# Key blocks loaded a period ahead: issued on GpSimd's queue, and at pieces 6 to 8 of the feed-forward

## The chip, the cores and the metric

The kernel runs on one core of a Trainium2 chip. The metric is the device time of one execution in microseconds. A core has engines that work side by side and meet through semaphores: TensorE (PE in the profile, its weight loads PEld), VectorE (DVE), ScalarE (ACT), GpSimd (POOL) and SyncE (SP). Each of them works its own list of instructions in order. SP does nothing but issue DMAs; ACT and POOL issue some too, between their computing instructions.

## The reference

Two stages. The first is a gated linear attention (delta rule) over 4 batches, 8 heads, 768 positions and head dimension 48, the second a feed-forward layer on the 3072 tokens that it gives.

```python
k_n = k / (np.linalg.norm(k, axis=-1, keepdims=True) + 1e-06)
for t in range(S):
    y[:, :, t] = einsum('bhd,bhde->bhe', q[:, :, t], state)
    v_old = einsum('bhde,bhd->bhe', state, k_n[:, :, t])
    state = state + beta_t * einsum('bhd,bhe->bhde', k_n[:, :, t], v[:, :, t] - v_old)
x = y.transpose(0, 2, 1, 3).reshape(B * S, H * D)          # 3072 x 384
h = np.maximum(np.maximum(x @ w1, x @ w2), x @ w3)         # 3072 x 768
out = h @ w_out                                            # 3072 x 384
```

The weights come as 64-bit floats and are turned to 32 bits on the chip.

## The kernel before

The positions are cut into 12 chunks of 64. A chunk has two units (two batches each), so there are 24 units, and a group is 4 units, that is two chunks: six groups, and six token tiles of 512. Within a chunk the recurrence becomes small matrix products: transposed keys and queries of a unit (`turn`, later `turn_blocks`), their products (`gram`), a triangular solve that VectorE does row by row for a whole group (`solve`, L569 and L573), and then the steps that carry the state from chunk to chunk (`old_k`, `old_q`, `new`, `step`, `to_y`).

The order of all work is written out by hand. The feed-forward of token tile m (`ffn(m)`) is a generator that yields after each of its pieces: for m of 1 to 5, pieces 0 to 11 are the hidden layer (6 blocks of two products, p_h, L927), and 12 to 19 are the four output blocks (p_o, L959, each with a copy o_sb on ACT and two stores on SP, L968). After each piece the loop at the end of the kernel calls `links`, which looks up in the table `LINKS` what else is emitted there for the groups behind: letters name functions, digits the unit or chunk. One pass of that loop, one m, is called a period here.

These letters matter for what follows:

- `y1`, `x1`, `w1`, `X1`: the attention output of a period's second chunk. `to_y` makes y (L813 on DVE), `y_blocks` stores it to a scratch tensor in DRAM (two DMAs on SP, L843), `read_y` reads it back rearranged into the tile qall (four DMAs on SP, L854), and `turn_y` transposes it on DVE into xt (L865). The first product p_h of the next period reads xt. `y0` to `X0` are the same for the first chunk.
- `L3`, `N0`, `N1`, `N2`: `load_blocks` for the four units of a group. It loads 32-row blocks of k and of q into two tiles, each after a small memset on GpSimd (L395), with 8 DMAs of 48 KB for k and 8 for q (L400). `N0` to `N2` serve the group after the next, `L3` the next one. The k blocks are issued by SP, the q blocks by GpSimd. Units whose number leaves 2 by division by 4 use the tiles kmore; the other units share five buffers named turned.
- `t0` to `t3`: `turn_blocks`, the DVE transposes (L416) that read these tiles and free their buffers.
- `P0`, `P1`: `prep_values`, a GpSimd multiplication of the values v_t (L292), which `old_k` of the next period needs (L755).
- `g0` to `g3`: after the product, part of the result goes to DRAM (at_d, L472, on SP) and comes back as x_bl (L519, on SP) for the next solve.

`N0` to `N2` do something only in the periods m=1 and m=2; in m=3 the group that they would serve no longer exists, while everything else of m=3 is as in m=2. The units 12 to 14 are loaded by direct calls in the first feed-forward, not by `N`.

SP's list in the second half of period m=1 has this order: x_bl, 8 key blocks of N0, y_x of the first chunk, qall, 8 key blocks of N1, two output stores, 8 key blocks of N2, y_x of the second chunk, two output stores, qall, four output stores, then the result of the solve (L595, L604).

Of the kernel before, what the change touches and what calls it, by code (L numbers as in the profile page):

```python
# [21 lines left out]
def kernel(  # L22
# [31 lines left out]
    nc = tc.nc  # L54
# [73 lines left out]
    def load_k(n, queues=one_queue):  # L128
        load(k, kpad[place(n)], n, queues)

    def load_q(n, queues=one_queue):
        load(q, qpad[n % NQ], n, queues)

    def load_v(c, queue=nc.sync):
        vts[c] = work.tile([128, 2, H, D], FP32, name="v_t", bufs=3)
        for bb in range(2):
            queue.dma_start(
                out=vts[c][rows(bb)].rearrange("p g h d -> p (g h) d"),
                in_=v[2 * bb : 2 * bb + 2, :, c * C : (c + 1) * C, :].rearrange(
                    "b h p d -> p (b h) d"  # L140
                ),
            )
# [66 lines left out]
    def fetch(queue=nc.scalar):  # L209
        if fetched[0] < len(pieces):  # L210
            _, src, (a, b) = pieces[fetched[0]]
            st = work.tile([128, 2 * 384], U32, name="w_bits", bufs=5)
            queue.dma_start(
                out=st.rearrange("p (a b) -> p a b", a=a), in_=src
            )
            staged.append(st)
            fetched[0] += 1
# [79 lines left out]
    def prep_values(c):  # L297

        scale(c, nrms.pop(c))
# [49 lines left out]
    def turn(n, parts=(0, 1), copy=nc.scalar.copy):  # L349

        if n not in kqts:
            if n == 6:
                kqts[n] = work.tile([128, KT, TOK], FP32, name="xt").rearrange(
                    "p k t -> p (k t)"
                )[:, 0 : NP * 4 * C].rearrange(
                    "p (j b i t) -> p j b i t", b=2, i=2, t=C
                )
            else:
                kqts[n] = work.tile([128, NP, 2, 2, C], FP32, name="kqt", bufs=6)
        kqt = kqts[n]  # L360
        p_t = ps_two("p_t")
        for i in parts:
            src = (kpad[place(n)], qpad[n % NQ])[i]
            for j in range(NP):
                nc.tensor.transpose(
                    p_t[:, i, j * 128 : (j + 1) * 128],
                    src[:, 2 * j : 2 * j + 2],
                    ident,
                )
        some = slice(parts[0], parts[-1] + 1)  # L370
        copy(  # L371
            kqt.rearrange("p j b i t -> p i (j b) t")[:, some],
            p_t.rearrange("p i (x t) -> p i x t", t=C)[:, some],
        )
# [6 lines left out]
    TURNED = 32 + NP * 2 * D + 16  # L381
    turned = {}

    def load_blocks(n):
        c, g = divmod(n, 2)
        for i in range(2):
            if n % 4 == 2:
                t = kmore[i].rearrange("p a h d -> p (a h d)")[:, 0 : 2 * TURNED]
                t = t.rearrange("p (b x) -> p b x", b=2)
            else:  # L390
                t = work.tile(
                    [128, 2, TURNED], FP32, name="turned", tag="w_bits", bufs=5
                )
            turned[n, i] = t
            nc.gpsimd.memset(t[:, :, TURNED - 48 : TURNED], 0.0)  # L395
            for bb in range(2):
                for par in range(2):
                    for db in range(2):
                        p0, at = DP * par + 32 * db, 32 * (1 - db)
                        (nc.sync, nc.gpsimd)[i].dma_start(  # L400
                            out=t[p0 : p0 + 32, bb, at : at + NP * 2 * D].rearrange(
                                "p (j x) -> p j x", j=NP
                            ),
                            in_=(k, q)[i][
                                2 * bb + g, :, c * C : (c + 1) * C, :
                            ].rearrange(
                                "(j two) (r tb) d -> two r j (tb d)", two=2, tb=2
                            )[par],
                        )
# [21 lines left out]
    def gram(n, parts=(0, 1), queues=one_queue, copy=nc.scalar.copy, later=False):  # L431
        kqt, g = kqts[n], n % 2
        p_g = ps_two("p_g")

        whole = len(parts) == 2 and not g
        for j in range(NP):
            for par in range(2):
                for bb in range(2):
                    kq = kqt[dims(par), j, bb ^ g]
                    for i in (0,) if whole else parts:  # L440
                        c0 = j * 128 + i * C
                        nc.tensor.matmul(  # L442
                            p_g[
                                rows(bb ^ (g * i)), par, c0 : c0 + C * (1 + whole)
                            ],
                            kq[:, 0],
                            kq if whole else kq[:, i],
                        )
        p_v = p_g.rearrange("p two (j i t) -> p two j i t", j=NP, i=2)
        if 1 in parts:  # L450
            pt = pts[n] = square("pt")
            if later:
                copy(by_par(pt), p_v[:, :, :, 1])
            else:
                masked(pt, p_v[:, :, :, 1])
        if 0 not in parts:
            return
        at = ats[n] = square("at")
        copy(by_par(at), p_v[:, :, :, 0])
        if queues:  # L460
            to_dram(n, queues)
# [511 lines left out]
    def some(gen, n):  # L973
        for _ in range(n):
            if next(gen, gen) is gen:
                break
# [72 lines left out]
    for c in range(2):  # L1049
# [29 lines left out]

    LINKS = {  # L1080
        0: "k0 q0 t0 L3", 1: "g0 t1", 2: "g1 t2", 3: "z0 d0 g2", 4: "z1 d1 t3",
        5: "j0 g3", 6: "j1", 7: "u0", 8: "s0", 9: "y0 N0", 10: "k1 q1 x0",
        11: "w0 N1 V0", 12: "u1", 13: "K0 K1 N2", 14: "y1 x1 X0 V1", 15: "s1 w1",
        16: "K2 K3 P0", 18: "X1 P1",
    }
    EARLY_LINKS = {
# [15 lines left out]
        e=halves_z, f=halves_u, d=turn_t1,  # L1102
    )
    MADE = dict(V=load_v, P=prep_values)
    UNIT = dict(t=turn, g=gram, K=load_k, L=load_blocks)
    OF_KEYS = dict(S=lambda n: some(solving, n), T=lambda n: turn(n, (1,)), P=lambda n: gram(n, (1,)))

    def links(m, names):
        for name in names.split():
            f, i = name[0], int(name[1])  # L1110
            if f in RECURS and m < GROUPS:
                RECURS[f](2 * m + i)
            elif f in MADE and m + 1 < GROUPS:
                MADE[f](2 * (m + 1) + i)
            elif f in UNIT and m + 1 < GROUPS:
                UNIT[f](4 * (m + 1) + i)
            elif f == "N" and m + 2 < GROUPS:
                load_blocks(4 * (m + 2) + i)

    def queries(names):  # L1120
        for name in names.split():
            f, n = name[0], int(name[1])
            if f not in OF_KEYS:
                links(0, name)
                continue
            OF_KEYS[f](n)
            if f == "T" and n + 3 < 11:
                load_q(n + 3)
# [4 lines left out]
    for i, _ in enumerate(ffn(0)):  # L1133
        if i - 1 in CONVERTED:
            fetch(nc.sync)
        queries(FIRST.get(i, ""))
        links(1, EARLY_LINKS.get(i, ""))
        if i in CONVERTED:
            some(conv, 1)
        if i in (4, 5, 6):  # L1140
            some(solving, (4, 2, 1)[i - 4])
        if i in (5, 7):
            prep_values(i // 2)
        if 7 <= i < 11:
            load_k(i + 1)
        if i == 0:
            load_v(3)
        if i == 12:
            load_q(11)
        if i in (10, 18):  # L1150
            load_v(4 + i // 18)
        if i == 18:
            blocks(2)
        if i == 21:
            solving = solve(2)
            some(solving, 1)
        if i in (22, 25):
            prep_values(4 + i // 25)
        if 21 < i < 27:
            some(solving, 3)  # L1160
        if i >= 27:
            some(solving, 4 if i < 30 else 5)
        if i in (27, 28, 29):
            load_blocks(i - 15)
        if i in (18, 19, 20, 22, 25, 27):
            less_first((18, 19, 20, 22, 25, 27).index(i))
        if 27 <= i < 30:
            turn_first((2 * (i - 27), 2 * (i - 27) + 1))


    RECURS.update(x=y_blocks, w=read_y, X=turn_y)
    UNIT.update(t=turn_blocks, K=lambda n: load_k(n, (nc.scalar, nc.scalar)))
    MADE.update(V=lambda c: load_v(c, nc.scalar))
# [45 lines left out]
```

## Time and profile before

| | |
|---|---|
| median of three runs | 565.05 us (562.16, 565.05, 565.74) |
| profiled execution, its own time | 563.47 us |
| profiled execution, span | 561.6 us |
| PE busy | 512.9 us (91%) |
| DVE busy | 312.8 us (56%) |
| ACT busy | 154.7 us (28%) |
| POOL busy | 127.6 us (23%) |
| mean granted TensorE clock | 0.95 |

The profile is one execution. Its times are microseconds from the start of the span. A group row gives an engine, an operation and its tiles, with the number of instructions and the busy time. In a timeline, a line is a run of like instructions: start, duration, engine, source line, tiles, count, and in brackets how long the engine had stood idle before, and whom it waited for. "PEclk" is the share of full speed that the clock of TensorE was granted. Rows of SPq, POOLq and ACTq are DMA issues or waits of those queues.

### The profile page before, as it was taken

The page shows a single profiled execution, that of the slowest core. Times are in us where ns is not written, and L with a number is a line of the kernel's source. Part 1 is how long each engine was busy: PE and PEld are TensorE (multiplying, and loading weights), DVE is VectorE, ACT ScalarE, POOL GpSimd, SP SyncE. Part 2 cuts the span into 40 slices and gives each one's busy share as a digit, 9 for nine tenths or more (in the row PEclk, how much of TensorE's full clock was granted, in tenths as well). Part 3 has the DMA queues.
Part 4 walks back from the last instruction along what each step waited for, and adds up shares of the span by engine and source line. Part 5 has one row for each costly group of instructions (what it writes and reads, how often), then busy time and mean ns, then how long its engine had stood idle before and what let it go on. Part 6 is the DMA issues. An engine that isn't in the chain of part 4 may idle for free.

```text
span 561.6 us, 18516 instructions
## 1 busy us (share of the span) xinstructions
PE 512.9 (91%) x8096; PEld 313.5 (56%) x8096; DVE 312.8 (56%) x694; ACT 154.7 (28%) x285; POOL 127.6 (23%) x219
## 2 busy tenths in 40 slices
PE   6568878899899999999599999599999999999996
PEld 5457667766446555556255556255565555654453
DVE  6878898668898350588163688262798212101000
ACT  4555455393303233210024200124201231011100
POOL 6215236144490533011066011030011000000000
PEclk9855799999989999999799999799999999999999
DMA  8884556975035744057474267551165400130001
GB/s 114 176 163 113 110 145 143 186 158 130 2 78 114 159 85 111 8 123 145 114 138 80 68 132 145 117 98 29 50 137 115 91 2 30 45 91 7 0 19 37
DMA packets 147455, 53.48 MB, mean 95 GB/s; under 512 B 131696, under 2 KB 143792, under 8 KB 147376
## 3 DMA queue, kind: packets, MB, share of 16 engines
q1 hardware_dynamic: 116784, 42.37, 35.0%
q10 hardware_dynamic: 27264, 5.11, 5.0%
q0 software_dynamic: 3328, 4.83, 3.9%
q8 instruction: 63, 1.03, 0.8%
q14 instruction: 16, 0.13, 0.1%
HBM read 39.17 MB, written 13.11 MB: 93 GB/s over the span
## 4 chain that ended last, share of the span: by engine, by line
PE 64%; DVE 15%; DMA 9%; SPq 5%; issue 3%; ACT 3%; POOL 0%; DVEq 0%; ACTq 0%; POOLq 0%
PE p_h L927 32%; PE p_o L959 15%; DMA y_x<-y 5%; PE p_g L442 3%; DVE tmp L569 3%; SPq L118 2%; DVE y_bl L573 2%; PE p_m L907 2%; SPq L854 2%; PE p_k L743 2%; PE p_j L726 2%; PE p_y L811 1%; PE p_q L743 1%; PE p_u L771 1%; PE p_s L793 1%
## 5 line engine op out<-in xcount | busy, mean ns | idle before, releaser
L927 PE MATMUL p_h<-xt,w_sb 128*128 128x512 f32 (+1 forms) x522 | 227.7, 578 | 18.1 <-DVE tmp L569 12.5
L927 PEld LDWEIGHTS p_h<-xt,w_sb 128*128 128x128 f32 x522 | 97.1, 197 | 103.1 <-issue 94.4
L959 PE MATMUL p_o<-wo_sb,h 128*128 128x384 f32 x288 | 99.4, 490 | 0.0
L941 DVE TENSOR_TENSOR h<-h,p_h 128x512 f32<-128x512 f32 (+1 forms) x48 | 29.6, 617 | 86.2 <-PE p_h L927 86.2
L959 PEld LDWEIGHTS p_o<-wo_sb,h 128*128 128x128 f32 x288 | 53.5, 190 | 35.9 <-issue 2.4
L569 DVE TENSOR_TENSOR tmp<-x_bl,y_bl 128x31 f32<-128x31 f32 (+20 forms) x139 | 52.6, 379 | 3.9
L573 DVE TENSOR_TENSOR y_bl<-y_bl,tmp 128x31 f32<-128x31 f32 (+20 forms) x139 | 48.6, 350 | 4.8
L292 POOL TENSOR_TENSOR v_t<-v_t,nrm 128x768 f32<-128x768 f32 x12 | 18.6, 1556 | 142.8 <-DMA v_t<-in_v_dram 75.8
L965 ACT COPY o_sb<-p_o 128x384 f32<-128x384 f32 x24 | 11.5, 478 | 130.8 <-PE p_o L959 86.0
L937 ACT ACTIVATE h<-p_h 128x512 f32<-128x512 f32 x30 | 17.9, 597 | 90.2 <-PE p_h L927 88.8
L959 PE MATMUL p_o<-w_sb,xt 128*128 128x384 f32 x120 | 42.0, 486 | 0.0
L400 POOL DMA_DIRECT2D turned<-in_q_dram x72 | 39.1, 551 | 3.0 <-POOL turned L395 3.0
L442 PE MATMUL p_g<-kqt 48*64 48x64 f32 (+1 forms) x1216 | 29.2, 237 | 10.6 <-DVE nt_bl L268 3.8
L442 PEld LDWEIGHTS p_g<-kqt 48*64 48x64 f32 x1216 | 24.3, 137 | 18.1 <-ACT kqt L371 7.8
L959 PEld LDWEIGHTS p_o<-w_sb,xt 128*128 128x128 f32 x120 | 22.8, 190 | 15.9
L426 DVE TENSOR_TENSOR pt<-p_g,mask 128x512 f32<-128x512 f32 x22 | 15.2, 690 | 24.1 <-PE p_g L442 23.9
L865 DVE STREAM_TRANSPOSE xt<-qall 128x768 f32<-128x768 f32 x8 | 9.7, 1212 | 25.6 <-DMA qall<-y_x 25.6
L236 POOL TENSOR_SCALAR mant<-mant 128x384 f32<-128x384 f32 x24 | 13.5, 562 | 43.3 <-ACT mant L232 43.3
L755 DVE TENSOR_TENSOR v_t<-v_t,p_k 128x768 f32<-128x768 f32 x11 | 10.4, 949 | 22.4 <-PE p_k L743 22.4
L799 DVE TENSOR_TENSOR st<-st,p_s 128x768 f32<-128x768 f32 x11 | 10.5, 951 | 21.1 <-PE p_s L793 21.1
L259 POOL TENSOR_TENSOR w_sb<-mant,up 128x384 int32<-128x384 int32 x18 | 17.9, 996 | 12.7 <-DVE mant L255 12.7
L395 POOL MEMSET turned<- 128x96 f32 x18 | 3.1, 187 | 77.3 <-DVE kqt L416 49.8
(147 smaller groups left out, 579.8 us busy)
## 6 DMA issues: line engine op xcount, KB each, us to landing
w_bits<-in_moe_w_dram SPq DMA_DIRECT2D x18, 384.0 KB, 4.7
out_dram<-o_sb SPq DMA_DIRECT2D x48, 96.0 KB, 2.2
turned<-in_q_dram POOLq DMA_DIRECT2D x72, 48.0 KB, 2.5
turned<-in_k_dram SPq DMA_DIRECT2D x72, 48.0 KB, 3.1
y_x<-y SPq DMA_DIRECT2D x16, 192.0 KB
qall<-y_x SPq DMA_DIRECT2D x32, 96.0 KB, 2.5
kpad<-in_k_dram ACTq DMA_DIRECT2D x28, 96.0 KB, 3.3
at_d<-at SPq DMA_DIRECT2D x80, 32.0 KB, 1.9
```

The source lines that it names most:

```text
L259: nc.gpsimd.tensor_tensor(out=dst.bitcast(I32), in0=mant_v.bitcast(I32), in1=up_v, op=ALU.add)
L292: nc.gpsimd.tensor_tensor(out=vts[c], in0=vts[c], in1=nrm[:, :, :, None].to_broadcast([128, 2, H, D]), op=ALU.mult,)
L400: (nc.sync, nc.gpsimd)[i].dma_start(out=t[p0 : p0 + 32, bb, at : at + NP * 2 * D].rearrange("p (j x) -> p j x", j=NP), in_=(k, q)[i][2 * b ...
L426: engine.tensor_tensor(out=by_par(t), in0=of, in1=mask[:, None, None, :].to_broadcast([128, 2, NP, C]), op=ALU.mult,)
L442: nc.tensor.matmul(p_g[rows(bb ^ (g * i)), par, c0 : c0 + C * (1 + whole)], kq[:, 0], kq if whole else kq[:, i],)
L569: nc.vector.tensor_tensor(out=t_v, in0=row.to_broadcast(t_v.shape), in1=column.to_broadcast(t_v.shape), op=ALU.mult,)
L573: nc.vector.tensor_tensor(out=rest, in0=rest, in1=t_v, op=ALU.subtract)
L743: nc.tensor.matmul(p_b[rows(bb), par, c0 : c0 + D], kqt[g][dims(par), j, bb ^ g, i], st[dims(par), bb ^ g, g, j],)
L927: nc.tensor.matmul(p_h, w_sb[i][:, t, f * 128 : (f + 1) * 128], xt[:, t, lo : lo + w], start=(t == 0), stop=(t == KT - 1),)
L937: nc.scalar.activation(out=h, in_=p_h, func=mybir.ActivationFunctionType.Relu)
L941: nc.vector.tensor_tensor(out=h, in0=h, in1=p_h, op=ALU.max)
L959: nc.tensor.matmul(p_o, stays, moves, start=(n == 0), stop=(n == len(terms) - 1))
```

## The change

`load_blocks` takes the queue for its key blocks as an argument, with GpSimd's as the default. The calls for the units 12 to 14 and the `L` entries pass SP's, as it was. The `N` entries take the default, and move from pieces 9, 11 and 13 to pieces 6, 7 and 8.

```diff
-    def load_blocks(n):
+    def load_blocks(n, queue=nc.gpsimd):
...
-                        (nc.sync, nc.gpsimd)[i].dma_start(
+                        (queue, nc.gpsimd)[i].dma_start(
...
-        5: "j0 g3", 6: "j1", 7: "u0", 8: "s0", 9: "y0 N0", 10: "k1 q1 x0",
-        11: "w0 N1 V0", 12: "u1", 13: "K0 K1 N2", 14: "y1 x1 X0 V1", 15: "s1 w1",
+        5: "j0 g3", 6: "j1 N0", 7: "u0 N1", 8: "s0 N2", 9: "y0", 10: "k1 q1 x0",
+        11: "w0 V0", 12: "u1", 13: "K0 K1", 14: "y1 x1 X0 V1", 15: "s1 w1",
...
-    UNIT = dict(t=turn, g=gram, K=load_k, L=load_blocks)
+    UNIT = dict(t=turn, g=gram, K=load_k, L=lambda n: load_blocks(n, nc.sync))
...
-            load_blocks(i - 15)
+            load_blocks(i - 15, nc.sync)
```

In the program as built, SP's list loses 48 DMA issues (24 in each of the periods m=1 and m=2) and GpSimd's gains them: in each N unit its order becomes memset, 8 key DMAs, memset, 8 query DMAs. The lists of PE, DVE and ACT are the same, instruction for instruction.

## The prediction, made before the changed kernel ran

> **What bounds the kernel now.** I read the page first: PE is busy 512.9 of 561.6 us, so what counts is where it is not. After 150 us the slices show full rows except two, and the timeline of PE says what stands there (start, duration, then the idle time before it):
>
> ```profile
> 274.73 5.25 PE L927 MATMUL p_h<-xt,w_sb 128*128 128x512 f32 x6 [6.36 <-DVE tmp L569]
> ...
> 358.07 4.55 PE L927 MATMUL p_h<-xt,w_sb 128*128 128x512 f32 x6 [6.19 <-DVE tmp L569]
> ...
> 434.35 2.74 PE L927 MATMUL p_h<-xt,w_sb 128*128 128x512 f32 x6
> ```
>
> These are the first p_h of the periods m=2, 3 and 4. Before two of them PE stands still for 6.36 and 6.19 us, and then the same six matmuls take 5.25 and 4.55 us where they take 2.74 at the third boundary. Windows laid on the first gap and behind it (PE busy, ..., PEclk, DMA share, GB/s) tell why:
>
> ```profile
> 268.40:274.70 6.30, 0.00 (x0) 0.00 (x0) 1.30 (x2) 0.48 (x1) 0.00 (x0) 0.85 0.49 118
> 274.70:280.00 5.30, 5.27 (x10) 1.94 (x14) 0.65 (x3) 0.00 (x0) 0.00 (x0) 0.53 0.52 124
> 280.00:315.00 35.00, 35.00 (x756) 19.69 (x757) 15.77 (x35) 12.69 (x21) 18.49 (x39) 1.00 0.55 114
> ```
>
> The clock falls while PE idles, and comes back only after some 5 us of work. The named releaser (tmp) is merely the neighbour of what p_h reads, xt (L865), which waits for qall. So, SP's timeline at the first boundary:
>
> ```profile
> 244.85 3.60 SPq L854 DMA_DIRECT2D qall<-y_x  x4
> 248.76 6.41 SPq L400 DMA_DIRECT2D turned<-in_k_dram  x8
> 255.28 1.16 SPq L968 DMA_DIRECT2D out_dram<-o_sb  x2
> 256.55 4.63 SPq L400 DMA_DIRECT2D kmore<-in_k_dram  x8
> 261.60 1.18 SPq L843 DMA_DIRECT2D y_x<-y  x2
> 262.88 1.64 SPq L968 DMA_DIRECT2D out_dram<-o_sb  x2
> 268.73 2.55 SPq L854 DMA_DIRECT2D qall<-y_x  x4
> ```
>
> and DVE's, the y that y_x stores and the xt that p_h reads:
>
> ```profile
> 252.84 0.95 DVE L813 TENSOR_TENSOR y<-qs,p_y 128x768 f32<-128x768 f32 x1 [0.17 <-PE p_y L811]
> ...
> 273.39 1.20 DVE L865 STREAM_TRANSPOSE xt<-qall 128x768 f32<-128x768 f32 x1 [7.40 <-DMA qall<-y_x]
> ```
>
> y is there at 253.79, its store is issued at 261.60. For those 7.8 us SP is busy issuing the key blocks of N1 and N2. Period m=3 has no N and is otherwise alike; there SP goes
>
> ```profile
> 415.09 1.15 SPq L968 DMA_DIRECT2D out_dram<-o_sb  x2
> 419.95 1.16 SPq L843 DMA_DIRECT2D y_x<-y  x2
> 422.17 1.15 SPq L968 DMA_DIRECT2D out_dram<-o_sb  x2
> 427.26 2.79 SPq L854 DMA_DIRECT2D qall<-y_x  x4
> ```
>
> with y done at 419.92, the store issued at once, xt at 432.03, and no gap. That is a control inside the trace.
>
> **What the Trainium skill says.** "TensorE: Matmul & The Clock Gate", What's actually happening: after an idle window of about 3.4 us the array runs at half clock, until it has worked for about as long again. The trace agrees: 0.53 granted after 6.36 us idle. "DMA: Bandwidth & Descriptors", Anatomy of one DMA: a semaphore wait happens on the issuing sequencer, so what is behind it in the list waits too; that agrees with the list of SP above. The same page, SWDGE vs HWDGE vs iDMA: for a DMA issued from GpSimd the descriptors are made by GpSimd's own cores, for SP by hardware, which is set up faster. The trace has the same blocks on both: q on GpSimd 548 ns an issue and 2.5 us to land, k on SP 430 ns (median) and 3.1 us; GpSimd's is no slower here in landing. "SBUF — State Buffer", Who interferes with whom: VectorE in a two-port mode locks GpSimd out, and GpSimd's descriptors with it. The trace shows none of it: GpSimd's 72 issues into turned last 548 at least, 548 in the median and 617 ns at most, beside a working DVE.
>
> **The change, part by part.**
>
> *SP loses 24 key issues in m=1 and in m=2.* New chain at the first boundary: y done 253.79; y_x issued at once, 1.18, so 255.0 (qall is through at 248.45, and the output stores before it need an o_sb that ACT has copied by 248.93). It lands 5.95 us after the end of issue, as now (262.78 to 268.73; 6.15 in m=3): 261.0. The output stores between need o_sb at 256.0 and hide in that. qall 2.55 to 2.79: 263.7. It lands and releases DVE 2.1 us later, as now (271.28 to 273.39): 265.8. DVE's solve steps ahead of L865 end at 265.98, as now. xt 266.0 to 267.2, PE 0.14 later (274.59 to 274.73): 267.35. PE's last p_o ends at 268.37, by then 1.0 us late for xt. At the second boundary y is done at 337.29; the same durations give PE 350.8, its p_o ends at 351.88, cover 1.1 us. So both idle times go: 6.36 + 6.19 = 12.55. The clock does not fall: against the 2.77 us of six warm p_h in the chain of waits, 5.25 - 2.77 = 2.48 and 4.55 - 2.77 = 1.78 go too. **Sum 16.8 us.**
>
> *GpSimd gains them.* From GpSimd's timeline:
>
> ```profile
> 206.70 4.33 POOL L400 DMA_DIRECT2D turned<-in_q_dram  x8 [0.36 <-POOL turned L395]
> ...
> 211.62 4.33 POOL L400 DMA_DIRECT2D kmore<-in_q_dram  x8 [0.29 <-POOL kmore L395]
> 246.55 1.73 POOL L292 TENSOR_TENSOR v_t<-v_t,nrm 128x768 f32<-128x768 f32 x1 [30.60 <-DVE tmp L569]
> ```
>
> 24 issues more at 0.548 are 13.2 us, so N2 ends near 229 at the latest instead of 216, and P0 starts at 246.5 behind 30.6 idle us. In m=2 it ends near 320 and P0 starts at 330.08. Cost nothing; without that cover each microsecond would still have to go past P0 to L755 in the next period.
>
> *New waits.* GpSimd's key memset and DMAs stand ahead of the query ones; N1's second tile waits for t3 as it does now (206.16), with N2 alone behind it. The q blocks come 4.3 to 13 us later, but t0 first reads them in the next period (DVE 282.06).
>
> *Pieces 6 to 8.* GpSimd has nothing else between pieces 6 and 13, and its waits are for buffers, not for pieces; for its q blocks the place is worth nothing. The key transfers move from 220-261 to about 193-225, where at_d, x_bl and ut travel. x_bl is the nearest: issued at 306.95, 4.5 us to land, read at 313.84, cover 2.4; the key blocks of N0 follow it on SP now (307.59), so it is not newly crowded. I take nothing; the bound is 0 to 2 us per period, none below nothing.
>
> *What is late next.* With the gap gone, the solve's result goes out behind the last output stores, as in m=3, where it left 1.95 us after PE's start (436.30); ut follows at +5.1 to +10.1, L3's key blocks to about +14.4, landed +17; t3 reads them at +19.4 (296.58 - 274.73 - 2.48). Cover 2.4 us.
>
> **Sum.** The profiled execution took 563.47 us (561.6 span): 563.47 - 16.8 = 546.7. The median of the runs is 1.6 above it, which gives 548.2. I forecast 548.0.
>
> **Rivals.**
>
> *The cover is thinner than worked out.* For: xt comes only 1.0 us ahead of PE, and y_x or qall may slow by 1 to 3 us. Against: m=3 has the same stores, K and V transfers and no gap. Idle of 1 to 3 us at each boundary, with up to the 4.3 us of clock lost again: 551 to 557.
>
> *The store was held by something else, or the queue change leaves it held.* For: six other DMAs stand near. Against: all stand in m=3 too. It gives 562 to 566.
>
> *GpSimd becomes the bound.* Place: its list from N0 to P0, which DVE's L755 needs at about 272 in the new time (281.19 less 8.84). From 193.2, 48 issues and some 5 us of memsets and P0 fit if an issue takes less than (272 - 193.2 - 5) / 48 = 1.54 us. Above that, each period grows by 48 times the excess. At 1.8 us, 2 x 48 x 0.26 = 25 us more: 573, slower. The lock-out would do that; the price is 3.3 times the 548 ns seen in all issues, so unlikely.
>
> **How the numbers follow.** Forecast 0.78 (545 to 551), thin cover 0.12 (551 to 557), held otherwise 0.04, GpSimd the bound 0.06. 1% is about what a measurement of this kernel tells from no change; 565.05 less 1% is 559.4. So faster 0.89, within 1% 0.05, slower 0.06. The range takes the forecast with the spread of the runs before (up to 3 below), and most of thin cover: 545 to 555.
>
> **What would show it.** Right: y_x (L843) within 0.2 us of y (L813) in m=1 and m=2; the first p_h of m=2 and m=3 without idle time and 2.8 us long; PEclk 1.00 through both boundaries; in each of the two periods GpSimd's 24 key and 24 query issues of N at about 0.55 us each, all before P0. Wrong: POOL issues well over 0.55 us, L865 still idle for qall by more than 1 us, or a new wait of L569 for x_bl or L416 for turned.

## The result, and the profile after

The changed kernel takes 546.26 us in the median of four runs (545.70 to 550.48), the kernel before beside it 563.61 (561.87 to 565.74): ratio 0.971, 95% interval 0.964 to 0.977. A second set on another occasion gave 546.32, ratio 0.971 (0.964 to 0.979). The profiled execution took 545.86 us, its span is 544.1. Single executions more than 1.5% above the fastest of their kernel are left out of the medians below.

The timeline of PE after, at the starts of the periods m=2, 3 and 4 (start, duration):

```profile
267.97 2.74 PE L927 MATMUL p_h<-xt,w_sb 128*128 128x512 f32 x6
...
342.44 2.74 PE L927 MATMUL p_h<-xt,w_sb 128*128 128x512 f32 x6
...
416.91 2.74 PE L927 MATMUL p_h<-xt,w_sb 128*128 128x512 f32 x6
```

No bracket stands behind any of them: PE comes without a pause from the last p_o, and the first p_h is as short as the third was before. Windows laid around the first two boundaries show PE busy throughout, and the clock at 1.00 (the columns are the stretch, its length, the busy time of PE, PEld, DVE, ACT and POOL, the clock, the DMA share and GB/s):

```profile
262.00:272.00 10.00, 10.00 (x118) 5.77 (x120) 5.46 (x18) 1.55 (x3) 0.00 (x0) 1.00 0.40 90
336.50:346.50 10.00, 10.00 (x120) 5.77 (x121) 5.36 (x18) 1.56 (x3) 0.00 (x0) 1.00 0.50 109
```

SP's timeline at the first boundary, and DVE's y and xt:

```profile
248.71 1.15 SPq L968 DMA_DIRECT2D out_dram<-o_sb  x2
253.58 1.16 SPq L843 DMA_DIRECT2D y_x<-y  x2
255.79 1.17 SPq L968 DMA_DIRECT2D out_dram<-o_sb  x2
260.81 2.81 SPq L854 DMA_DIRECT2D qall<-y_x  x4
```

```profile
252.59 0.95 DVE L813 TENSOR_TENSOR y<-qs,p_y 128x768 f32<-128x768 f32 x1
...
265.77 1.22 DVE L865 STREAM_TRANSPOSE xt<-qall 128x768 f32<-128x768 f32 x1
```

y is there at 253.54 and its store goes out at 253.58, where it had waited 7.8 us. L865 does not wait for qall any more. GpSimd's timeline holds the key blocks, a long way ahead of P0:

```profile
212.26 4.34 POOL L400 DMA_DIRECT2D kmore<-in_k_dram  x8 [0.30 <-POOL kmore L395]
...
217.08 4.34 POOL L400 DMA_DIRECT2D kmore<-in_q_dram  x8 [0.29 <-POOL kmore L395]
246.60 1.48 POOL L292 TENSOR_TENSOR v_t<-v_t,nrm 128x768 f32<-128x768 f32 x1 [25.18 <-DMA v_t<-in_v_dram]
```

**A finer measure.** The first 185 us, which the change leaves alone, end anywhere from 183.0 to 189.0 us in the profiles; what lies behind came out the same to 0.01 us in both kernels that were profiled twice (the changed one, and the queue alone below). So below I also give the *stretch*, from the first p_k of period m=1 (184.80 before, 184.56 after) to the first p_h of m=4 (434.35 and 416.91): 249.55 us before, 232.35 after, 17.20 less. The second profile of the changed kernel gives 232.35 again.

### The profile page after: what moved, and what is told of

It reads as the page before. It is cut to its first block, busy times and chain, and to the rows that moved or that the text cites. A ratio compares the mean times of both kernels' runs of the same rounds, so it can differ in the third digit from the quotient of the medians.

```text
span 544.1 us, 18513 instructions
## 1 busy us (share of the span) xinstructions
PE 508.8 (94%) x8096; PEld 313.3 (58%) x8096; DVE 313.4 (58%) x694; ACT 154.9 (28%) x285; POOL 153.4 (28%) x267
## 4 chain that ended last, share of the span: by engine, by line
PE 83%; DVE 11%; issue 2%; ACT 2%; DMA 1%; SPq 0%; POOL 0%; DVEq 0%; ACTq 0%; POOLq 0%
PE p_h L927 36%; PE p_o L959 25%; PE p_g L442 4%; PE p_y L811 2%; PE p_k L743 2%; PE p_m L907 2%; DVE tmp L569 2%; PE p_q L743 2%; PE p_u L771 2%; PE p_s L793 2%; PE p_j L726 2%; PE p_z L712 1%; PE p_t L365 1%; DVE y_bl L573 1%; ACT ut L588 1%
## 5 line engine op out<-in xcount | busy, mean ns | idle before, releaser
L927 PE MATMUL p_h<-xt,w_sb 128*128 128x512 f32 (+1 forms) x522 | 222.3, 567 | 5.8 <-DVE h L941 3.6
L927 PEld LDWEIGHTS p_h<-xt,w_sb 128*128 128x128 f32 x522 | 95.6, 193 | 87.0 <-issue 77.9
L573 DVE TENSOR_TENSOR y_bl<-y_bl,tmp 128x31 f32<-128x31 f32 (+20 forms) x139 | 51.2, 368 | 4.8
L569 DVE TENSOR_TENSOR tmp<-x_bl,y_bl 128x31 f32<-128x31 f32 (+20 forms) x139 | 51.2, 368 | 3.9
L442 PE MATMUL p_g<-kqt 48*64 48x64 f32 (+1 forms) x1216 | 30.3, 243 | 11.7 <-DVE nt_bl L268 4.2
L442 PEld LDWEIGHTS p_g<-kqt 48*64 48x64 f32 x1216 | 25.2, 142 | 19.3 <-issue 8.3
L959 PEld LDWEIGHTS p_o<-w_sb,xt 128*128 128x128 f32 x120 | 22.8, 190 | 15.9
L799 DVE TENSOR_TENSOR st<-st,p_s 128x768 f32<-128x768 f32 x11 | 10.5, 950 | 21.1 <-PE p_s L793 21.1
L755 DVE TENSOR_TENSOR v_t<-v_t,p_k 128x768 f32<-128x768 f32 x11 | 10.5, 950 | 18.2 <-PE p_k L743 15.5
L459 ACT COPY at<-p_g 128x512 f32<-128x512 f32 x21 | 12.3, 586 | 27.1 <-DVE pt L426 24.8
L776 ACT COPY u<-p_u 128x768 f32<-128x768 f32 (+1 forms) x12 | 9.3, 771 | 36.5 <-PE p_u L771 36.5
```

Source lines behind the costliest of these rows:

```text
L442: nc.tensor.matmul(p_g[rows(bb ^ (g * i)), par, c0 : c0 + C * (1 + whole)], kq[:, 0], kq if whole else kq[:, i],)
L569: nc.vector.tensor_tensor(out=t_v, in0=row.to_broadcast(t_v.shape), in1=column.to_broadcast(t_v.shape), op=ALU.mult,)
L573: nc.vector.tensor_tensor(out=rest, in0=rest, in1=t_v, op=ALU.subtract)
L927: nc.tensor.matmul(p_h, w_sb[i][:, t, f * 128 : (f + 1) * 128], xt[:, t, lo : lo + w], start=(t == 0), stop=(t == KT - 1),)
L959: nc.tensor.matmul(p_o, stays, moves, start=(n == 0), stop=(n == len(terms) - 1))
```

## The experiments

Theory A is that of the prediction: SP issued the key blocks of N1 and N2 between qall of the first chunk and y_x of the second, and that held the store. The rivals are named in each expectation. A kernel's "ratio" is its time over that of the kernel before, run beside it, with the 95% interval in brackets.

| kernel | median us | stretch us | idle at the two boundaries |
|---|---|---|---|
| before | 562.7 to 563.9 | 249.55 | 6.36, 6.19 |
| changed | 546.3 | 232.35 | none |
| place alone | 561.2 | 247.58 | 4.63, 4.30 |
| queue alone | 545.7, 547.7 | 232.35, 232.36 | none |
| only N2 to GpSimd | 550.5 | 233.85 | 0.40, 0.64 |
| only N0 to GpSimd | 564.8 | 249.02 | 5.98, 6.20 |
| PE filled | 561.3 | 246.55 | (filled) |
| changed, small issues on SP | 568.9 | 253.41 | 8.20, 9.13 |
| changed, small issues on GpSimd | 557.9 | 245.05 | 0.53, none |
| changed, all keys on GpSimd | 548.2 | 233.00 | 0.02, 0.15 |
| place alone, V and K off ACT | 551.4 | 236.67 | 0.98, 1.35 |
| changed, V and K off ACT | 553.1 | 236.93 | 1.30, 1.30 |

**The queue alone.** The table LINKS as before, with the new default queue:

```diff
-        5: "j0 g3", 6: "j1 N0", 7: "u0 N1", 8: "s0 N2", 9: "y0", 10: "k1 q1 x0",
-        11: "w0 V0", 12: "u1", 13: "K0 K1", 14: "y1 x1 X0 V1", 15: "s1 w1",
+        5: "j0 g3", 6: "j1", 7: "u0", 8: "s0", 9: "y0 N0", 10: "k1 q1 x0",
+        11: "w0 N1 V0", 12: "u1", 13: "K0 K1 N2", 14: "y1 x1 X0 V1", 15: "s1 w1",
```

> Key blocks on GpSimd's queue, N units at pieces 9, 11 and 13 as before: the queue alone. Theory A: GpSimd has nothing else there, so the place is worth nothing to it, 545 to 548 us, as the changed kernel. Rival C (the pieces 6 to 8 make part of the gain, as the transfers must be out of the way): some 3 to 8 us slower than the changed kernel.

545.68 us, ratio 0.967 (0.962 to 0.972); run once more beside the changed kernel,

> The queue alone again, beside the changed kernel on one chip. Theory A: GpSimd issues the blocks at the same moments in both, within 1% of the changed kernel, 545 to 549. Rival C: 3 to 8 us slower.

> The changed kernel as it is, on the same chip as its variants: 545 to 549.

547.67 against 546.32 us, and a stretch of 232.36 against 232.35. The medians differ by 0.25%, the stretches by 0.01 us: the move to pieces 6 to 8 is worth nothing once the keys are on GpSimd, and rival C falls.

**The place alone.** N at pieces 6 to 8, the keys still on SP: the second half of the diff without the first.

> The N units at pieces 6 to 8 with their key blocks still on SP: the place alone. Theory A (what cost the time is that SP issued the key blocks of N1 and N2 between qall of the first chunk and y_x of the second): SP issues all 24 right behind x_bl, 24 x 0.6 = 14 us, from 219.9 to 234, before y_x of the first chunk at 237; the two gaps go, 546 to 548 us. Rival B (the queue makes the gain, the keys must leave SP): the time stays near 563.

561.24 us, ratio 0.994 (0.992 to 0.997): my expectation was wrong. SP's timeline of this kernel, and from its table of waits the longest of that queue between 215 and 280 (us in total, times, longest):

```profile
219.71 8.63 SPq L400 DMA_DIRECT2D turned<-in_k_dram  x16
228.46 14.82 SPq L400 DMA_DIRECT2D kmore<-in_k_dram  x8
243.37 1.24 SPq L843 DMA_DIRECT2D y_x<-y  x2
250.19 3.61 SPq L854 DMA_DIRECT2D qall<-y_x  x4
```

```profile
SPq L400 <- DMA v_t<-in_v_dram: 10.7, 2, 10.5
```

Sixteen key issues take 8.6 us as expected; the last eight take 14.8, because one of them waits 10.5 us for a load of V with which it has nothing to do. ACT issues that load, behind its copy at 238.23:

```profile
238.23 0.80 ACT L763 COPY qs<-p_q 128x768 f32<-128x768 f32 x1 [1.45 <-PE p_q L743]
238.24 1.34 ACTq L137 DMA_DIRECT2D v_t<-in_v_dram  x2
```

A completion semaphore is a counter by which a DMA tells that its data has landed. The program as built gives the DMAs of SP and ACT eight of them in turn, in one common order (in the trace, number 100 and numbers 102 to 108), and an issue waits until the DMA that had its semaphore last has landed; GpSimd's DMAs have eight of their own (111 to 118). In this kernel two of N2's keys come one turn behind the two halves of that V load: both loads and both keys carry the numbers 107 and 102 in the trace. So y_x of the *first* chunk goes out 6.3 us behind its y, and its qall is late. That holds two things:

```profile
257.07 1.26 SPq L968 DMA_DIRECT2D out_dram<-o_sb  x2
258.43 1.32 SPq L843 DMA_DIRECT2D y_x<-y  x2
```

```profile
SPq L968 <- DMA qall<-y_x: 3.2, 1, 3.2
```

```profile
271.27 1.20 DVE L865 STREAM_TRANSPOSE xt<-qall 128x768 f32<-128x768 f32 x1 [1.84 <-DMA qall<-y_x]
272.62 5.46 PE L927 MATMUL p_h<-xt,w_sb 128*128 128x512 f32 x6 [4.63 <-DVE tmp L569]
```

The first xt stops DVE for 4.90 us, and the solve steps behind it are late. And an output store that shares a semaphore with that qall waits 3.2 us for it, so that y_x of the second chunk too goes out 5.0 us behind its y (258.43 against 253.40). The second wait ends last: L865 stands 1.84 us for qall, and PE 4.63. To test this, the loads of V and K were taken off ACT in both kernels:

```diff
-    UNIT.update(t=turn_blocks, K=lambda n: load_k(n, (nc.scalar, nc.scalar)))
-    MADE.update(V=lambda c: load_v(c, nc.scalar))
+    UNIT.update(t=turn_blocks, K=lambda n: load_k(n, (nc.gpsimd, nc.gpsimd)))
+    MADE.update(V=lambda c: load_v(c, nc.gpsimd))
```

> The place alone once more (N at pieces 6 to 8, its keys on SP), with the loads of V and K that ACT issued in the periods m=1 to m=4 moved to GpSimd's queue, so that no issue of SP stands behind one of ACT's through a shared completion semaphore. Theory E (what failed in e1_place was only that SP's last key issues waited for a V load that ACT issues at 238, because the two queues take turns on eight semaphores): SP is through with the keys by 234, y_x of both chunks goes out when y is there, both gaps go: 545 to 549. Rival B (keys on SP cost the gain in any place): near 561, as e1_place.

> The control for it: the changed kernel with V and K moved to GpSimd's queue in the same way. If moving V and K gains nothing by itself, 545 to 549, as the changed kernel and as e9_place_lanes; if it brings something of its own, e9_place_lanes has to be read against this one.

551.35 (ratio 0.980, 0.972 to 0.987) and 553.09 us (0.982, 0.975 to 0.989); stretches 236.67 and 236.93. SP with the keys at pieces 6 to 8, now without the foreign wait:

```profile
222.88 7.63 SPq L400 DMA_DIRECT2D turned<-in_k_dram  x16
230.63 4.64 SPq L400 DMA_DIRECT2D kmore<-in_k_dram  x8
238.12 1.24 SPq L843 DMA_DIRECT2D y_x<-y  x2
...
254.43 1.16 SPq L843 DMA_DIRECT2D y_x<-y  x2
```

The eight issues are back at 4.64 us, y_x at y. Both kernels are slower than forecast, but against each other they are even. Theory E stands: keys on SP are harmless in a place that is early enough, if no semaphore ties them to a load of ACT's. The place leaves less room than that sounds: in m=2 SP's keys waited 3.2 us for earlier keys, and y_x of the first chunk went out 4.0 us behind y there (317.73 against 313.78), which cost nothing.

Moving V and K costs some 4.6 us of the stretch by itself (236.93 against 232.35): PE idles 1.0 to 1.35 us at all three boundaries, that of m=4 too. The traces point to GpSimd and DVE. In GpSimd's list P0 now stands behind the four K loads (L118), and it runs back to back with P1 while DVE is at the solve steps ahead of xt; one of these steps takes 3.98 us instead of 0.41. First the changed kernel with V and K moved, then a solve step of the changed kernel beside its P1 (256.74):

```profile
263.52 2.91 POOL L292 TENSOR_TENSOR v_t<-v_t,nrm 128x768 f32<-128x768 f32 x2
262.71 3.98 DVE L573 TENSOR_TENSOR y_bl<-y_bl,tmp 128x231 f32<-128x231 f32 x1
...
256.82 1.66 DVE L573 TENSOR_TENSOR y_bl<-y_bl,tmp 128x240 f32<-128x240 f32 x1
```

In the changed kernel P0 comes earlier (246.60), where DVE has time left before y. This is read from the traces; no run here moved P0 and P1 alone.

**Only N2, only N0.** Places as before, one unit's keys to GpSimd:

```diff
-                load_blocks(4 * (m + 2) + i)
+                load_blocks(4 * (m + 2) + i, nc.gpsimd if i == 2 else nc.sync)
```

and `i == 0` in the other.

> Places as before, only N2's key blocks on GpSimd; N1's stay on SP between qall and y_x. Theory A: SP is through with N1 and the output stores at 256.4, so y_x goes out 2.6 us late against a cover of 1.0: each gap is 1.6 us instead of 6.3. If so short an idle leaves the clock up, the loss against the changed kernel is 3.2 us (549.5); if the clock falls all the same, 7.5 us (554).

> Places as before, only N0's key blocks on GpSimd. Theory A: N0 was issued at 220 to 224, 13 us ahead of y_x of the first chunk, so it held nothing: as the kernel before, 563.6. A theory in which the gain is the number of issues taken off SP gives a third of it, 558.

N2: 550.45 us, ratio 0.976 (0.970 to 0.982). y_x was 1.5 us late (255.79 against a y of 254.32), not 2.6. PE's first p_h of m=2 and m=3:

```profile
269.30 2.81 PE L927 MATMUL p_h<-xt,w_sb 128*128 128x512 f32 x6 [0.40 <-DVE tmp L569]
344.65 2.81 PE L927 MATMUL p_h<-xt,w_sb 128*128 128x512 f32 x6 [0.64 <-DVE tmp L569]
```

At the first boundary about 1.1 us of the lateness was cover and 0.40 came out as idle time; at the second y_x was 1.1 us late, and 0.64 came out, since it also took longer to land. The clock stayed up. N0: 564.80 us, ratio 1.002 (1.000 to 1.004), no change. A third of the issues bought next to nothing (0.5 us of the stretch), another third nearly all (15.7 of 17.2): what counts is where they stand.

**Issue time or data.** The changed kernel with 26 DMAs of 512 bytes on SP where N1 and N2 had stood:

```diff
+    tiny = const.tile([128, 104], FP32, name="tiny")
...
+    def issues(lo, n, queue):
+        for x in range(lo, lo + n):
+            queue.dma_start(out=tiny[0:32, 4 * x : 4 * x + 4], in_=k[0, 0, 0:32, 0:4])
...
-        11: "w0 V0", 12: "u1", 13: "K0 K1", 14: "y1 x1 X0 V1", 15: "s1 w1",
+        11: "w0 I0 V0", 12: "u1", 13: "K0 K1 I1", 14: "y1 x1 X0 V1", 15: "s1 w1",
...
+            elif f == "I" and m + 2 < GROUPS:
+                issues((0, 15)[i], (15, 11)[i], nc.sync)
```

> The changed kernel with 26 further DMA issues of 512 bytes each on SP in the periods m=1 and m=2, 15 where N1 stood and 11 where N2 stood (0.43 us each, 11.2 us in all, as long as the 16 key issues took there). Theory A (SP's issue time holds the store): the gaps come back, 560 to 564 us. Rival D (the key blocks' data slowed y_x and qall on the DMA engines): 26 x 512 bytes move next to nothing, the time stays at 546 to 548.

568.88 us, slower than forecast, ratio 1.011 (1.008 to 1.015). SP and PE at the first boundary:

```profile
250.13 8.22 SPq L1113 DMA_DIRECT2D tiny<-in_k_dram  x15
258.47 1.15 SPq L968 DMA_DIRECT2D out_dram<-o_sb  x2
259.66 5.53 SPq L1113 DMA_DIRECT2D tiny<-in_k_dram  x11
265.29 1.18 SPq L843 DMA_DIRECT2D y_x<-y  x2
```

```profile
278.43 4.48 PE L927 MATMUL p_h<-xt,w_sb 128*128 128x512 f32 x6 [8.20 <-DVE tmp L569]
```

Next to no data, and the gap is back, larger than before: the 26 issues took 13.75 us in all rather than 11.2. One of them takes 0.42 us in the median, as I had reckoned, but 0.05 us lie between two, and a few are longer (up to 1.49). y_x went out 9.6 us behind y. Rival D falls: time that SP spends on issues is enough to hold the store, whatever they move. Nor were y_x and qall slow beside the keys: from the end of y_x's issue to qall's first issue it is 5.95 us in the kernel before and 6.07 in the changed one.

In the kernel before, though, SP's time was not issuing alone. Its table of waits between 244 and 265 has, for the issues ahead of y_x,

```profile
SPq L400 <- DMA turned<-in_k_dram: 1.4, 2, 0.8
SPq L400 <- DMA kpad<-in_k_dram: 0.7, 1, 0.7
```

and 0.4 us of y_x itself: 2.5 us in which SP waited for earlier transfers to land, by the same eight semaphores. At the second boundary (327 to 348) such waits come to 4.0 us. So the 7.8 us for which the store stood behind the keys are issues in the main and such waits for the rest; the change took both away.

**The clock's share.** The kernel before, with 11 matmuls (22 records in the profile) whose result is not used in PE's pause:

```diff
+        if m < 3:
+            busy(11, wo_sb[:, 0])
```

> The kernel before, with 11 further matmuls (identity by 384 columns, result unused, about 5.4 us) on PE at the end of the periods m=1 and m=2, where PE stood still. Theory A: the wait for xt stays, the clock does not fall, and the first six p_h take 2.8 us instead of 5.25 and 4.55: 563.6 - 4.3 = 559.3. If the long first p_h came from something else than the idle PE, 563.6 or more.

561.25 us, ratio 0.994 (0.992 to 0.997); the stretch is 3.0 us shorter. PE:

```profile
270.59 7.26 PE L990 MATMUL p_w<-wo_sb,ident 128*128 128x384 f32 x22
277.68 2.74 PE L927 MATMUL p_h<-xt,w_sb 128*128 128x512 f32 x6
```

The first p_h takes 2.74 us though it waited for xt as long as before: the 5.25 was the fallen clock. The gain stays below 4.3 because the filler took 7.26 us and not 5.4, and so ran about 0.9 and 1.3 us past xt. Against the kernel before, with the gain of the clock counted out, p_h came 0.6 and 0.7 us later; with these 1.3 us the clock's share is 4.3, as forecast.

**GpSimd as the bound.** The changed kernel with 80 DMAs of 128 bytes behind N2 on GpSimd's queue:

```diff
                 load_blocks(4 * (m + 2) + i)
+                if i == 2:
+                    issues(0, 80, nc.gpsimd)
```

> The changed kernel with 80 further DMA issues of 128 bytes each on GpSimd behind N2 in the periods m=1 and m=2, 80 x 0.55 = 44 us. The slower rival's place and price: in m=1 GpSimd is through at 265, P0 and P1 by 269, L755 needs them at 271.8: nothing. In m=2 it is through at 354, P0 at 355.6, where L755 stood at 346.3: PE waits some 9 us once and loses up to 2.5 us of clock: 555 to 558. If P0 were needed earlier than worked out, 60 us or more in all.

557.92 us, ratio 0.991 (0.988 to 0.994), 11.6 above the changed kernel. DVE and PE behind the second boundary:

```profile
362.53 0.95 DVE L755 TENSOR_TENSOR v_t<-v_t,p_k 128x768 f32<-128x768 f32 x1 [14.07 <-POOL v_t L292]
```

```profile
364.64 2.21 PE L442 MATMUL p_g<-kqt 48*64 48x128 f32 x32 [9.28 <-DVE kqt L416]
366.78 4.09 PE L927 MATMUL p_h<-xt,w_sb 128*128 128x512 f32 x6
```

The bound is where the rival put it: P0 (361.01) holds L755, L755 holds the transposes, and PE loses 9.3 us and its clock. In m=1 the same issues cost next to nothing (0.53). In m=2 they took 48.4 us (312.59 to 361.0, 9.2 us of waits among them), and 14.07 came out as a wait of L755, of which it spends 4.16 in the changed kernel too, for p_k. There N2 ends at 310.03 and L755 starts at 346.38, so P0, which takes 1.48, has a cover of some 35 us.

**All keys on GpSimd.** L3 and the units 12 to 14 as well:

```diff
-    UNIT = dict(t=turn, g=gram, K=load_k, L=lambda n: load_blocks(n, nc.sync))
+    UNIT = dict(t=turn, g=gram, K=load_k, L=load_blocks)
...
-            load_blocks(i - 15, nc.sync)
+            load_blocks(i - 15)
```

> The changed kernel with all key blocks on GpSimd, those of L3 and of the units 12 to 14 too. Theory A: these issues hold nothing on SP that is late, and L3's two tiles land by +14.5 instead of +17 us against a need at +19.4: 545 to 548, as the changed kernel. If SP is still short behind the second qall, 1 to 3 us faster.

548.23 us (three executions, 544.19 to 551.71), ratio 0.974 (0.966 to 0.982), stretch 233.00: no gain over the changed kernel. SP isn't short elsewhere.

## Why the prediction was right

*What the gap is worth.* Forecast 16.8 us; medians 17.35, profiled executions 17.6, stretch 17.20. The waiting part (12.55) and the clock part (4.26) are both borne out, the second by the filled pause (3.0 us, and 1.3 that the filler ran on). The 0.4 us missing from the sum is PE's overlap: without a pause the first p_h starts 0.17 us before the modelled end of the last p_o, at each boundary.

*The chain.* y_x was forecast at y and came 0.04 us after it; xt was forecast for 266.0 to 267.2 and stood at 265.77 to 266.99, with PE's p_o ending at 268.14. The cover of 1.0 us is what the N2 experiment used up at the first boundary before idle time appeared. My words for the old state were too simple: in the 7.8 us SP was not only "busy issuing", it also waited for earlier transfers (2.5 us of SP's time at the first boundary, 4.0 at the second). As the keys left SP, these waits went too, and the forecast did not depend on the difference.

*GpSimd.* I let N2 end "near 229 at the latest"; it ended at 221.4, since the key issues fill the 8.4 us in which GpSimd had stood waiting for t3. Issues stayed at 0.55 us.

*The place.* "Worth nothing" holds: 232.36 and 232.35. That the reverse also fails, the place without the queue, I had not seen, and my reason for expecting it to work was wrong: I counted issue times on SP and left out that an issue can wait for a transfer of another queue.

*What is late next.* The solve's result went out 1.96 us after PE's start (269.93; forecast 1.95), L3's keys were issued by +15.9 (forecast +14.4), t3 read them at +19.3 (forecast +19.4). No new wait.

*Starting point.* The forecast of 548.0 was made against a median of 565.05; the kernel before now stands at 562.7 to 563.9. That is the rest of the difference to 546.3.

## What to carry to other kernels

A queue that only issues DMAs can still be the bound at one place: look for a store whose data is ready long before it is issued, and read what stands ahead of it in that queue's list. Prefetches that nobody needs for a period belong behind such stores or on another queue, and where issues stand matters more than how many there are. Before moving a prefetch earlier on the same queue, look at which transfers share its completion semaphores: a load issued late by another engine can hold it.

## What the runs showed of the hardware

- At the boundaries TensorE's clock survived idle times up to 1.35 us (place alone with V and K off ACT: the next six p_h in 2.81 us) and fell in those of 4.3 us and more (place alone: 5.46 us). The Trainium skill, "TensorE: Matmul & The Clock Gate", What's actually happening, puts the idle window at about 3.4 us, which agrees. But the length of a pause does not settle it alone. A pause in the part that all kernels have in common brought the clock down in the profile of the kernel before (first line; 0.50 granted from 156.8 to 160.1) and not in that of the changed one (second line; 1.00 throughout):

```profile
155.80 7.08 PE L927 MATMUL p_h<-xt,w_sb 128*128 128x512 f32 x12 [2.94 <-DVE h L941]
157.26 5.39 PE L927 MATMUL p_h<-xt,w_sb 128*128 128x512 f32 x12 [2.95 <-DVE h L941]
```

- An SP issue of 512 bytes took 0.42 us in the median, one of 48 KB 0.43: what a DMA costs its queue here is not its size.
- GpSimd's 144 issues of key and query blocks in the changed kernel took 548 to 617 ns; no lock-out by VectorE, as "SBUF — State Buffer", Who interferes with whom, describes for its two-port modes, shows in their length. One pause of 2.40 us between two of them (from 290.26) has no cause in the profile.
- The other way round GpSimd's P0 and P1 seem to hold VectorE: in the kernel before and the changed one each of the six between 185 and 440 us has a solve step beside it that is longer by 0.4 to 1.3 us.
- The part of an execution behind 185 us repeated to 0.01 us between two profiles of one kernel, while the part ahead of it ended anywhere from 183.0 to 189.0 in kernels that are alike up to there.
